# A chunked RWKV-7 recurrence with top-1 expert routing: blocks fetched unit by unit, triangular inversion spread over four slots, logits summed on GpSimd, late weights behind the second gather

## The chip, the cores and the metric

The kernel runs on one core of a Trainium2 chip. The metric is the device time of one execution in microseconds (us). The core has five instruction streams: PE (TensorE: matmuls, with PEld for its weight loads), DVE (VectorE), ACT (ScalarE), POOL (GpSimd) and SP (SyncE, which here only issues DMA transfers). Each stream works through its own instructions in order and waits where a result of another stream, or a transfer, is missing. All DMA transfers run on 16 shared DMA engines.

## The reference

First comes a linear recurrence over 768 tokens for 4 batches x 8 heads, with a state matrix of 40 x 40 for each, then a routed feed-forward layer over all 3072 tokens of width 320:

```python
for t in range(S):                       # 768 tokens; r, k, v, w, a, b: (4, 8, 768, 40)
    y[:, :, t] = einsum('bhd,bhde->bhe', rt, state)
    Sa = einsum('bhde,bhe->bhd', state, at)
    state = state * wt[:, :, None, :] - einsum('bhd,bhe->bhde', Sa, bt) \
            + einsum('bhd,bhe->bhde', vt, kt)
x = y as (3072, 320)
logits = x @ w_gate                      # 8 experts
expert_idx = argmax(logits); gate_w = softmax(logits)[expert_idx]
for e in range(8):                       # only the 80 tokens of largest gate_w are kept
    out[tok_idx] = gate_w[tok_idx] * (relu(x[tok_idx] @ w1[e]) @ w2[e])
```

Tokens that are not kept stay zero in the output.

## The kernel before

**Tiling.** The sequence is cut into 12 chunks of T = 64 tokens, the batches into 2 pairs: 24 *units*, taken in the order chunk by chunk, pair by pair. A unit holds 2 batches x 8 heads x 64 tokens. The states of the two pairs take turns, so unit n needs the state that unit n - 2 left. Four consecutive units (NG = 4) make a *group*; there are six. Inside a unit the recurrence is turned into matmuls. This needs the inverse of a triangular matrix for each head, in two diagonal blocks of C = 32 tokens; the part below the diagonal is done by a matmul (`below`).

**Ahead work.** What doesn't depend on the state is made seven units ahead (AHEAD = NG + 3). In the loop over n, m = n + 7 is the unit made ahead and o = n - 1 the unit that is finished. `decays`, `forward` and `backward` turn `w` into running products (a PE transpose, an ACT copy, DVE scans). `turned_a`/`decayed_a`, `doubled`/`inverted` and `operand` make the scaled factors. `system` multiplies them into `np`, and `system_kept` (L352) copies it to the tile `nt` on ACT, stores `nt` to the DRAM tensor `blocks` (two transfers, L355), and masks `nt` on POOL.

**Inversion of a group.** The inverses of a group's 4 x 16 head-chunks in 2 blocks are computed at once on DVE, one on each partition, with the 32 x 32 matrix along the free axis. Three steps lead there. `fetch(k)` (L365) reads the blocks of group k back from DRAM into `lt`, four transfers of 32 partitions each. `begin(k)` (L370) makes the start matrix `tt` with a mask on POOL. Thirty `step`s follow, two DVE instructions each (L381, L384). `end(k)` writes `tt` to the DRAM tensor `solved` (L387) and reads it back, transposed, as `dt` (L392). `diagonal` uses `dt` as matmul weights from the first unit of the next four slots on.

**Order of the work.** The order on each engine is written out by hand. Everything goes through `do`, which ties each new instruction to the one before it on the same engine, SP among them, so each engine's order is the order of the text. In the loop the places are, for unit n: `decays(m+1)`, `turned(o)`, `system(m)`, the scans, `together` (matmuls with v and with the state), `right`, `system_kept(m)`, the fetch (in n % 4 == 0 only, for the group just completed), `doubled`, `right_kept`, `turned_a(m+1)`, `lower(o)`, `diagonal(n, 0)`, `inverted(m+1)`, `reads_g`, `below`, then the list of inversion steps, `logits(o-1)`, `turned_r`, `diagonal(n, 1)`, `operand(m+1)`, `summed(o)` (which writes the new state at L522 and `xT` at L526), `logits_summed(o-1)`. Every input load is issued by SP right behind the operation that frees its single buffer (`raw_w`, `raw_a`, `raw_s`, `raw_r`; `v` has three).

The inversion steps wait in a list `steps` with a cost in us for each. `pause(steps, x)` takes steps from it until their costs exceed x. Before the change, `begin` stands in slot 0 of a group (n % 4 == 0), and `invert`, which fills the list, at the end of that slot; the steps then run in slots 1 and 2 (6.7 us each, besides 0.7 us earlier in each slot) and 3 (the rest). In the last group, where nothing is made ahead any more, the amounts are 9 and 5.5.

**Start.** `prepare` makes units 0 to 6 ahead before the loop. The first group's inversion runs there in full, with nothing else on DVE.

**Gate.** `logits` multiplies `xT` with a picking matrix that holds the gate weights, copies the result to `xb` and stores the token rows to `x_rows`; `logits_summed` adds its four parts (L552, DVE). `gate` turns four units of logits into probabilities; the largest 80 gate weights of each expert are found with lists of maxima on DVE.

**Routing and experts.** After the loop, POOL splits ids and gates into bf16 pieces (`pieces`), DVE and PE find each kept token's slot and row number, `keep_at_work` runs 40 filler matmuls (L146), and POOL gathers the rows of the first four experts (L932). SP loads the expert weights: experts 0 to 2 before that, then a small transfer `held`, which reads the row numbers `idx_g` (L983), then experts 3 to 7. Each expert is `tokens` (transposes, L942/L944), `first_half` (L955, L962), `second_half` (L972) and an indirect store (L975).

Of the kernel before, what the change touches and what calls it, by code (L numbers as in the profile page):

```python
# [18 lines left out]
def kernel(  # L19
# [26 lines left out]
    nc = tc.nc  # L46
# [19 lines left out]
    assert G * ZT == 512 and NG * 32 == 128 and E == 8 and 1 <= cap <= 128  # L66
# [66 lines left out]
    ones_b = const.tile([128, 128], BF16, name="ones_b")  # L133
    behind_b = const.tile([128, 128], BF16, name="behind_b")
    seg_t = const.tile([128, E, 2 * NM], F32, name="seg")
    seg = seg_t.rearrange("p e m -> p (e m)")
    iot = const.tile([128, 1, cap], F32, name="iot")


# [7 lines left out]

    nc.gpsimd.tensor_copy(ones_b, ones)
    nc.gpsimd.tensor_tensor(out=behind_b, in0=strict, in1=ones, op=Alu.subtract)
    nc.gpsimd.memset(seg_t, 1.0)  # L150
    nc.gpsimd.memset(seg_t[:, :, 0:1], 0.0)
    iot_i = const.tile([128, cap], I32, name="iot_i")
    nc.gpsimd.iota(iot_i, pattern=[[1, cap]], base=1, channel_multiplier=0)
    nc.gpsimd.tensor_copy(iot[:, 0, :], iot_i)


    with ExitStack() as p1:
# [202 lines left out]
        def fetch(k):  # L360
            inverse[k]["lt"] = lt = sb.tile([128, C * C], F32, name="lt", tag="lt")
            for i in range(Z):
                for j in range(NS):
                    m = block(i, j)
                    nc.sync.dma_start(lt[m].rearrange("p (s t) -> p s t", s=C),  # L365
                                      blocks[k, m, :, :, j * C : (j + 1) * C].rearrange("s u h t -> (u h) s t"))
# [183 lines left out]
        def logits_summed(n):  # L550
            i = share_of[n]
            nc.vector.tensor_reduce(logit[i][:, n - shares[i][0], :], of[n]["xb"][:, :, 2 * D :].rearrange("p g e -> p e g"),  # L552
                                    axis=AX, op=Alu.add)
            of[n].clear()
# [137 lines left out]
        def joined(n):  # L692
            do(operand, n)
            do(system, n)
            do(system_kept, n)

        def prepare(n, before=None, next_=True):
# [10 lines left out]
            if before is not None:  # L708
                do(system, before)
                do(system_kept, before)  # L710
            if next_:
# [11 lines left out]
        do(fetch, 0)  # L723
# [18 lines left out]
        for n in range(NU + 2):  # L742
# [24 lines left out]
            if coming:  # L767
                do(system_kept, m)
                if m % NG == NG - 1:
                    do(fetch, m // NG)  # L770
# [25 lines left out]
            if not coming:  # L796
                pause(steps, 9 if n % NG == 1 else 5.5 if n % NG == 2 else 100)
                pause(rounds_, LISTS.get(n, 0))
            elif n % NG == 0:
                do(begin, m // NG)  # L800
            else:
                pause(steps, 6.7 if n % NG < NG - 1 else 100)
# [218 lines left out]
```

## Time and profile before

| what | value |
|---|---|
| median of 3 runs | 620.11 us (618.28 to 622.42) |
| profiled execution | 620.17 us |
| its span, first to last instruction | 618.5 us |
| mean granted TensorE clock | 0.871 |
| busy: PE / PEld / DVE / ACT / POOL | 480.6 / 411.2 / 362.5 / 234.7 / 130.2 us |

Time by stage in the profiled execution (us from the start; clock is the granted share of TensorE's full clock):

| stage | from : to | length | PE busy | DVE busy | clock | DMA share |
|---|---|---|---|---|---|---|
| start, units 0 to 4 made ahead | 0 : 49.8 | 49.8 | 29.96 | 35.52 | 0.97 | 0.63 |
| first inversion, rest of the start | 49.8 : 98.8 | 49.0 | 16.93 | 30.45 | 0.55 | 0.52 |
| units n = 0 to 3 | 98.8 : 164.2 | 65.4 | 58.09 | 44.12 | 0.90 | 0.55 |
| n = 4 to 7 | 164.2 : 236.4 | 72.2 | 65.50 | 48.27 | 0.88 | 0.68 |
| n = 8 to 11 | 236.4 : 302.3 | 65.9 | 57.62 | 48.81 | 1.00 | 0.68 |
| n = 12 to 15 | 302.3 : 368.0 | 65.7 | 58.98 | 45.49 | 0.95 | 0.53 |
| n = 16 to 19 | 368.0 : 425.5 | 57.5 | 46.72 | 38.74 | 0.94 | 0.43 |
| n = 20 to 23 and the last reads | 425.5 : 476.5 | 51.0 | 43.90 | 29.02 | 0.97 | 0.18 |
| end of the gate | 476.5 : 497.5 | 21.0 | 5.80 | 18.39 | 0.58 | 0.08 |
| routing, first gather | 497.5 : 526.2 | 28.7 | 10.07 | 16.65 | 0.59 | 1.01 |
| first experts | 526.2 : 551.4 | 25.2 | 24.67 | 0.81 | 0.59 | 1.06 |
| remaining experts | 551.4 : 618.5 | 67.1 | 62.31 | 6.26 | 0.98 | 0.24 |

How to read it: a line of the trace gives the start, the length, the engine, the line of the kernel, the operation, and what it writes and reads; in brackets stand the idle time of the engine just before it and what ended that idle time. "SPq" is SP's queue of DMA issues; the length there is the time that the issue took, not the transfer. A matmul's end is modelled, so a busy PE isn't PE at its peak.

### The profile page before, as it was taken

The numbers are of one execution on the slowest core, as the hardware profiler recorded it, in microseconds if no ns is written. First come the engines' busy times: TensorE is split into PE (matmuls) and PEld (weight loads), VectorE is DVE, ScalarE is ACT, GpSimd is POOL, SyncE is SP. The second block draws the span as 40 slices with busy tenths as digits, with TensorE's granted clock in tenths as the row PEclk, the third lists the DMA queues.
The fourth block names the chain that finished last, engine by engine and source line by source line (L and its number), as shares of the span: only waits on it lengthen the run. The fifth ranks groups of instructions, "written<-read, shape, count | busy, mean of one in ns | idle before, by whom it ended". The sixth has DMA issues, their size and how long they took to land. (4 is left out here: it accounts for less than half of the span.)

```text
span 618.5 us, 25228 instructions
## 1 busy us (share of the span) xinstructions
PE 480.6 (78%) x11281; PEld 411.2 (66%) x11281; DVE 362.5 (59%) x870; ACT 234.7 (38%) x418; POOL 130.2 (21%) x171
## 2 busy tenths in 40 slices
PE   2874039978979898978998898599888205999996
PEld 1653037867869787877887787488777204877874
DVE  8766932678547874888567853988266984001010
ACT  2462015645654655655564554154445000000000
POOL 5022003222221412422231133021112012111011
PEclk9986557989996989999998899799999556579999
DMA  4587077535777658765766345125210179995000
GB/s 75 109 165 134 11 122 124 95 64 116 137 122 145 133 128 153 144 140 96 141 113 121 73 87 103 33 70 79 49 33 14 21 258 347 330 334 158 14 14 14
DMA packets 236033, 71.46 MB, mean 116 GB/s; under 512 B 217236, under 2 KB 228756, under 8 KB 235924
## 3 DMA queue, kind: packets, MB, share of 16 engines
q1 hardware_dynamic: 223728, 66.47, 49.6%
q10 hardware_dynamic: 11428, 1.73, 1.7%
q8 instruction: 89, 1.46, 0.9%
q0 software_dynamic: 768, 1.64, 0.9%
q14 instruction: 20, 0.16, 0.1%
HBM read 51.69 MB, written 18.12 MB: 113 GB/s over the span
## 5 line engine op out<-in xcount | busy, mean ns | idle before, releaser
L272 POOL TENSOR_SCALAR_AFFINE_SELECT side<-side 64x1024 f32<-64x1024 f32 x47 | 55.3, 1176 | 113.0 <-ACT side L500 111.7
L384 DVE TENSOR_TENSOR tt<-tt,tmp 128x30 f32<-128x30 f32 (+9 forms) x180 | 71.2, 396 | 6.6
L381 DVE TENSOR_TENSOR tmp<-tt,lt 128x30 f32<-128x30 f32 (+9 forms) x180 | 65.2, 362 | 14.5 <-POOL tt L370 9.3
L272 POOL TENSOR_SCALAR_AFFINE_SELECT nt<-nt 64x512 f32<-64x512 f32 x48 | 34.4, 717 | 139.6 <-ACT nt L352 138.3
L416 PE MATMUL yp<-rT,gT 64*64 64x64 f32 x768 | 30.6, 231 | 35.9 <-DVE lg L552 28.2
L416 PEld LDWEIGHTS yp<-rT,gT 64*64 64x64 f32 x768 | 27.7, 145 | 37.8 <-issue 35.6
L319 ACT COPY qd<-qt 128x1024 f32<-128x1024 f32 x24 | 25.3, 1053 | 71.6 <-DVE qt L305 68.1
L974 DVE TENSOR_SCALAR y<-yp,weight 80x320 f32<-80x320 f32 x8 | 4.4, 548 | 79.4 <-PE yp L972 79.4
L522 DVE TENSOR_TENSOR state<-yp,pt 64x320 f32<-64x320 f32 x44 | 21.4, 487 | 50.1 <-PE yp L518 49.8
L518 PE MATMUL yp<-side,scaled 128*64 128x128 f32 (+1 forms) x768 | 47.5, 279 | 2.2 <-POOL side L272 2.2
L245 PE MATMUL tp<-ident,raw_a 128*128 128x128 f32 x96 | 19.2, 333 | 35.4 <-DMA raw_a<-in_a_dram 35.0
L518 PEld LDWEIGHTS yp<-side,scaled 128*64 128x64 f32 x768 | 41.9, 143 | 3.9 <-POOL side L272 2.4
L298 DVE TENSOR_TENSOR_SCAN pt<-decay,begins 128x520 f32<-128x520 f32 x24 | 30.3, 1263 | 20.2 <-ACT decay L292 20.0
L453 PE MATMUL pr<-yy,dt 32*32 32x40 f32 x1536 | 39.0, 203 | 3.7 <-ACT yy L446 1.8
L453 PEld LDWEIGHTS pr<-yy,dt 32*32 32x32 f32 x1536 | 32.6, 111 | 10.9 <-issue 5.7
L972 PE MATMUL yp<-w,hT 128*80 128x320 f32 x128 | 38.5, 448 | 0.0
L245 PEld LDWEIGHTS tp<-ident,raw_a 128*128 128x128 f32 x96 | 12.4, 166 | 38.5 <-issue 34.7
L966 ACT ACTIVATE hT<-hp 128x320 f32<-128x320 f32 x16 | 6.1, 434 | 83.3 <-PE hp L962 83.3
L955 PEld LDWEIGHTS hp<-xe,w 128*128 128x128 f32 x256 | 36.2, 227 | 1.5 <-issue 0.2
L955 PE MATMUL hp<-xe,w 128*128 128x80 f32 x256 | 36.4, 311 | 0.0
L266 PE MATMUL sp<-ahT,sT 64*64 64x64 f32 x1536 | 32.7, 241 | 2.3 <-ACT sT L342 2.3
L404 PE MATMUL pr<-side,nt 64*64 64x40 f32 x768 | 33.8, 235 | 0.4 <-issue 0.4
(300 smaller groups left out, 998.9 us busy)
## 6 DMA issues: line engine op xcount, KB each, us to landing
w<-in_moe_w_dram SPq DMA_DIRECT2D x8, 1280.0 KB, 14.1
w<-in_moe_w_dram SPq DMA_DIRECT2D x8, 1024.0 KB, 15.9
blocks<-nt SPq DMA_DIRECT2D x48, 128.0 KB, 2.5
raw_w<-in_w_dram SPq DMA_DIRECT2D x48, 80.0 KB, 3.2
raw_s<-in_b_dram SPq DMA_DIRECT2D x48, 80.0 KB, 2.9
raw_r<-in_r_dram SPq DMA_DIRECT2D x48, 80.0 KB, 3.1
side<-in_v_dram SPq DMA_DIRECT2D x48, 80.0 KB, 2.8
x_rows<-xb SPq DMA_DIRECT2D x48, 80.0 KB, 2.3
```

Source lines behind the costliest of these rows:

```text
L245: nc.tensor.transpose(p[:, g, :], t[:, g, :], ident)
L266: nc.tensor.matmul(p[i, q, z, g, :], lhsT=lhs[m, z, g, i], rhs=rhs[m, g, halves[z]], start=True, stop=True)
L272: nc.gpsimd.affine_select(out=o, in_=o, compare_op=Alu.is_gt, fill=0.0, base=0, pattern=[[0, o.shape[1]], [1, T]], channel_multiplier=-1)
L298: nc.vector.tensor_tensor_scan(flat(pt), flat(chunks(n)), flat(begins), 0.0, op0=Alu.mult, op1=Alu.add)
L381: nc.vector.tensor_tensor(out=tm, in0=t3[:, 0:i, i : i + 1].to_broadcast([128, i, n]), in1=l3[:, i : i + 1, i + 1 :].to_broadcast([128, i, ...
L384: nc.vector.tensor_tensor(out=t3[:, 0:i, i + 1 :], in0=t3[:, 0:i, i + 1 :], in1=tm, op=Alu.add)
L404: yield lambda h=h, z=z: nc.tensor.matmul(pr[halves[1 - z], h, :], lhsT=o["nt"][halves[z], z, of_head(n, h), :], rhs=vu[halves[z], z, h, 0:D],
L416: yield lambda z=z, g=g, m=m: nc.tensor.matmul(y[m, z, g, 0:T], lhsT=o["gT"][m, z, g, :], rhs=o["rT"][m, g, halves[z]], start=g == 0, stop ...
L453: nc.tensor.matmul(o["pr"][m, h, :], lhsT=dt_[m, (n % NG) * 2 * G + of_head(n, h), :], rhs=o["yy"][m, h, :], start=h == 0, stop=True, skip ...
L518: nc.tensor.matmul(o["y"][m, z, g, 0 : T if last else T + HB], lhsT=o["s"][:, z, 2 * g + q, :], rhs=x, start=False, stop=True, skip_group_ ...
L955: nc.tensor.matmul(hp[f // (FK // 2)][:, f % (FK // 2), :], lhsT=t1[:, i, f * 128 : (f + 1) * 128], rhs=xe[:, i, :], start=f % (FK // 2) = ...
L972: nc.tensor.matmul(yp, lhsT=hT[:, f, :], rhs=w2[:, f, :], start=f == 0, stop=f == FK - 1)
```

## The change

The change has five parts.

1. **Fetch by unit.** `fetch` now takes a unit n in place of a group. It reads that unit's quarter of the blocks into `lt` (eight partitions for each of four transfers), directly after `system_kept` of the same unit, in the start and in the loop. `lt` gets two buffers.
2. **Steps in four slots.** In slot 0, `invert` and `pause(steps, 3)` follow `begin` at once; slots 1 and 2 take 4.9 instead of 6.7. The last group's amounts become 8 and 5.
3. **Logits on POOL.** For the first 20 units `logits_summed` is two additions on POOL instead of one reduction on DVE.
4. **Constants.** `ones_b`, `behind_b`, `seg` and `iot`, which only the routing reads, are made on POOL after the loop, behind `pieces`, in a pool of their own (`gp`) that also holds `pieces` and `rest`.
5. **Late weights.** `held` reads the rows that the second gather delivered (`rows[1]`) instead of `idx_g`, so SP issues the weights of experts 3 to 7 only after that gather has landed. The fillers grow from 40 to 52.

```diff
-        def fetch(k):
-            inverse[k]["lt"] = lt = sb.tile([128, C * C], F32, name="lt", tag="lt")
+        def fetch(n):
+            k, u = n // NG, n % NG
+            if u == 0:
+                inverse[k]["lt"] = sb.tile([128, C * C], F32, name="lt", tag="lt", bufs=2)
             for i in range(Z):
                 for j in range(NS):
                     m = block(i, j)
-                    nc.sync.dma_start(lt[m].rearrange("p (s t) -> p s t", s=C),
-                                      blocks[k, m, :, :, j * C : (j + 1) * C].rearrange("s u h t -> (u h) s t"))
+                    x = m.start + 2 * G * u
+                    nc.sync.dma_start(inverse[k]["lt"][x : x + 2 * G].rearrange("h (s t) -> h s t", s=C),
+                                      blocks[k, m, u, :, j * C : (j + 1) * C].rearrange("s h t -> h s t"))
...
         def logits_summed(n):
             i = share_of[n]
-            nc.vector.tensor_reduce(logit[i][:, n - shares[i][0], :], of[n]["xb"][:, :, 2 * D :].rearrange("p g e -> p e g"),
-                                    axis=AX, op=Alu.add)
+            lg, x = logit[i][:, n - shares[i][0], :], of[n]["xb"][:, :, 2 * D :]
+            if n < NL:
+                part = sb.tile([128, G // 2, E], F32, name="part", tag="part")
+                nc.gpsimd.tensor_tensor(out=part, in0=x[:, 0 : G // 2], in1=x[:, G // 2 :], op=Alu.add)
+                nc.gpsimd.tensor_tensor(out=lg, in0=part[:, 0], in1=part[:, 1], op=Alu.add)
+            else:
+                nc.vector.tensor_reduce(lg, x.rearrange("p g e -> p e g"), axis=AX, op=Alu.add)
...
         # in joined(n) and, for `before`, in prepare(n, before):
             do(system_kept, n)
+            do(fetch, n)
...
         # in the start:
-        do(fetch, 0)
         do(begin, 0)
...
         # in the loop:
             if coming:
                 do(system_kept, m)
-                if m % NG == NG - 1:
-                    do(fetch, m // NG)
+                do(fetch, m)
...
             if not coming:
-                pause(steps, 9 if n % NG == 1 else 5.5 if n % NG == 2 else 100)
+                pause(steps, 8 if n % NG == 1 else 5 if n % NG == 2 else 100)
                 pause(rounds_, LISTS.get(n, 0))
             elif n % NG == 0:
                 do(begin, m // NG)
+                invert(m // NG)
+                pause(steps, 3)
             else:
-                pause(steps, 6.7 if n % NG < NG - 1 else 100)
+                pause(steps, 4.9 if n % NG < NG - 1 else 100)
...
-            if coming and m % NG == NG - 1:
-                invert(m // NG)
...
 +    ones_b = gp.tile([128, 128], BF16, name="ones_b")
+    behind_b = gp.tile([128, 128], BF16, name="behind_b")
+    seg_t = gp.tile([128, E, 2 * NM], F32, name="seg")
+    iot = gp.tile([128, 1, cap], F32, name="iot")
+    nc.gpsimd.tensor_copy(ones_b, ones)
+    nc.gpsimd.tensor_tensor(out=behind_b, in0=strict, in1=ones, op=Alu.subtract)
+    nc.gpsimd.memset(seg_t, 1.0)
+    nc.gpsimd.memset(seg_t[:, :, 0:1], 0.0)
+    nc.gpsimd.iota(iot_i, pattern=[[1, cap]], base=1, channel_multiplier=0)
+    nc.gpsimd.tensor_copy(iot[:, 0, :], iot_i)
...
-        keep_at_work(ps_l, "still", 40, late)
+        keep_at_work(ps_l, "still", 52, late)
...
-    held = nc.dram_tensor("held", (cap, E), I32, kind="Internal")
-    nc.sync.dma_start(held[:, :], idx_g)
+    held = nc.dram_tensor("held", (cap, E), F32, kind="Internal")
+    nc.sync.dma_start(held[:, :], rows[1][:, 0:E])
     for e in range(3, E):
         weights_of(e)
```

## The prediction

> **What bounds the kernel now.** I read the table of stages first, then the queue of SyncE in one group of units, then the chain around one fetch, then the tail. Unit n runs from one copy `yy<-pr` on ACT to the next; a unit with n divisible by 4 is slot 0 of its group. Columns of the stage table: start:end, length, then busy time (and count) of PE, PEld, DVE, ACT, POOL, granted clock, DMA share, GB/s.
>
> ```profile
> 250.60:269.20 18.60, 14.72 (x448) 13.18 (x448) 15.50 (x36) 9.30 (x16) 6.88 (x10) 1.00 0.66 135
> 269.20:286.00 16.80, 14.61 (x451) 12.80 (x448) 14.60 (x30) 9.34 (x16) 3.83 (x4) 1.00 0.64 132
> 286.00:300.40 14.40, 13.88 (x442) 12.37 (x442) 10.91 (x27) 8.41 (x16) 2.28 (x2) 1.00 0.64 132
> 300.40:315.80 15.40, 14.43 (x445) 12.61 (x445) 7.76 (x18) 10.46 (x19) 4.28 (x6) 1.00 0.71 116
> ```
>
> These are slots 1, 2, 3 and the next slot 0. Slots 1 and 2 carry most inversion steps, have DVE busy for 15 us and are 2 to 3 us longer; slots 3 and 0 stand at 14.4 and 15.4 us, near PE's own 14. A second limit shows only in the queue of SyncE (start, length, line, transfer):
>
> ```profile
> 264.88 1.24 SPq L548 DMA_DIRECT2D x_rows<-xb  x2
> 266.21 1.31 SPq L212 DMA_DIRECT2D raw_r<-in_r_dram  x2
> 267.63 2.07 SPq L212 DMA_DIRECT2D side<-in_v_dram  x2
> 269.79 0.59 SPq L660 DMA_DIRECT2D out_dram<-zero  x1
> 270.47 1.58 SPq L212 DMA_DIRECT2D raw_w<-in_w_dram  x2
> 272.15 1.26 SPq L355 DMA_DIRECT2D blocks<-nt  x2
> 273.50 1.71 SPq L212 DMA_DIRECT2D raw_a<-in_a_dram  x2
> 275.30 0.60 SPq L212 DMA_DIRECT2D raw_s<-in_k_dram  x1
> ```
>
> Each start is the end before it plus 0.1 us: SyncE issues 17 transfers a unit without a pause, about 0.8 us each with gaps, 13.0 to 13.7 us a unit. Slots 0 and 3 add the fetch and the `solved`/`dt` transfers. Over n = 8 to 11 (65.9 us) SyncE is short of work for under 5 us, all but 1.2 of it waits for transfers to land. It is already the fullest queue, and it runs late, as one fetch shows:
>
> ```profile
> 234.53 0.99 ACT L352 COPY nt<-sp 128x1024 f32<-128x1024 f32 x1
> 241.21 1.22 SPq L355 DMA_DIRECT2D blocks<-nt  x2
> 243.72 2.94 SPq L365 DMA_DIRECT2D lt<-blocks  x4
> 245.94 0.99 DVE L522 TENSOR_TENSOR state<-yp,pt 64x320 f32<-64x320 f32 x2 [5.73 <-PE yp L518]
> 249.83 1.76 POOL L370 TENSOR_SCALAR_AFFINE_SELECT tt<-lt 128x1024 f32<-128x1024 f32 x1 [9.56 <-DMA lt<-blocks]
> ```
>
> `nt` is ready at 235.5, its store is issued 5.7 us later, the fetch waits 1.3 us for the store to land, and `begin` on POOL starts at 249.83, **after** DVE's state update of that unit. Before the change nobody needs `begin` until slot 1.
>
> **The Trainium skill.** "DMA: Bandwidth & Descriptors", section "Two DMAs through the same engine are not ordered", says that a read of what another DMA wrote must wait at the issuing engine for the completion semaphore; the 1.3 us gap before 243.72 is that wait, with all of SyncE's queue behind it. Section "Issuing engines are not separate DMA queues" calls issue time usually small beside the transfer; here 17 issues fill a unit, so the trace decides. "TensorE: Matmul & The Clock Gate", Part 1, says that an idle window of some 3.4 us halves the clock; the trace agrees: 0.55 granted over 49.8 to 98.8 us, where PE is busy for 17 of 49 us.
>
> **The change, part by part.** The sum is made against the profiled execution: 620.17 us, span 618.5 and 1.7 around it; the median of the three runs is 620.11, the same.
>
> *Fetch by unit.* Per group, 4 fetch issues become 16, each of a quarter. Four issues took 2.13 to 2.96 us; from below, the first of each four takes 0.31, so 1.4 us. I take 2.3, since issue time hardly follows size (80 KB loads and 128 KB stores all take 0.6). The wait ahead was 1.3 to 2.8 us; I take 1.3. So 3.6 us of SyncE in each of slots 1, 2, 3, and nothing new in slot 0. Behind it stand `raw_a`, `raw_s`, `x_rows`, `raw_r`, `v`, `raw_w` and the next store; from the end of its issue to PE's use a load of `raw_a` has 3.4 us for n = 9 (248.1 to 251.5), 10.2 for n = 11 (275.2 to 285.4). SyncE's time for n = 8 to 11 becomes 65.9 - 1.2 + 3 x 3.6 = **75.5 us**.
>
> *Steps in four slots.* DVE spends 22.7 us a group on 60 step instructions (136 us over six groups). Spread evenly, a slot has 5.7 beside 6.1 of other DVE work, and slot 3 shows that 4.6 us of steps cost nothing: all four units would run at about 15.2 us, 60.8 a group, **5 us less** than 65.9. But slot 0's six steps stand in DVE's order ahead of the state update and now wait for `begin`. From the store's issue: 8.6 us to `begin` (241.21 to 249.83), less 0.8 for the smaller fetch, plus 1.4 for the mask with its memset of 0.15, plus 3.5 for six steps (the six equal-sized ones that end the first inversion): **12.9 us**. The state update came 4.7 us after that issue, so DVE is 8.2 us late; at n = 4, 12, 16 the same sum gives 9.4, 8.1, 8.3. Behind the waiting DVE are state, xT and the next scans; PE's next state matmuls wait for xT. Each us by which SyncE falls further behind is added; with units of 15.2 against SyncE's 16.7, 16.7 and about 23.7 (slot 3), it is 4 to 5 more, so a stall of 13.
>
> So the groups: n = 0 to 3 has no state update in slot 0 and a SyncE with 17 us idle, -2. n = 4 to 7: 60.8 + 13 = 74 to 75 against 72.2 (which held 13.7 us of half clock), +2.5. n = 8 to 11: 75.5 against 65.9, +9.6. n = 12 to 15: 60.8 + 13, and 3 for a PE that goes to half clock in the stall, against 65.7, +11. n = 16 to 19: stall 8.3, less 3 for steps moved out of n = 17 (20.6 us now), plus 3 of clock, +8. **Loop: +29.**
>
> *Start.* Units 0 to 3 are made every 5.9 us with SyncE busy for about 4.9; with 3.6 more they take 8.3. Three such intervals are +7, less 2.5 because only a quarter is fetched after the last: **+4.7** until `begin(0)`, and all that follows waits for it. The later fetches (units 4, 5) fall where SyncE waits from 61.7 to 77.4: nothing; without that cover 7.
>
> *POOL's constants.* Six instructions, 0.28 + 0.44 + 0.41 + 0.10 + 0.19 + 0.24 = 1.7 us, leave the start, where DVE's 8-element cast lasts 3.75 us, until POOL's memsets are over: **-1.5** (from 0 to -1.7). At the end they run from 499.9, and the first reader starts at 509.94: nothing.
>
> *Logits on POOL.* Two adds of at most 0.24 us (the row of `ids`) on a POOL that is 21% busy, read by the gate three units later: nothing. DVE loses 0.2 us in 20 units, inside the stalls: nothing.
>
> *Tail.*
>
> ```profile
> 516.91 6.45 PE L146 MATMUL still_p<-late 128*128 128x256 bf16 x40
> 526.23 0.33 PE L942 MATMUL xp<-ident,rows 80*128 80x80 f32 x2 [2.87 <-DMA rows<-x_rows,idx_g]
> 528.08 7.12 PE L955 MATMUL hp<-xe,w 128*128 128x80 f32 x32
> 553.11 3.69 PE L955 MATMUL hp<-xe,w 128*128 128x80 f32 x32
> ```
>
> The same 32 matmuls take 7.12 us, later 3.69: after the 2.87 us gap PE ran at half clock from 527.7 to 548.2. Twelve more fillers of 0.16 us last until 525.3. The gather took 6.75 us among weight loads against 3.7 when alone (the last one); with the late weights held back it lands 0.6 to 1.6 us earlier, so the gap is about nil: **-1.5**, and if the clock holds, half of 20.5 us more: **-10**. The late weights start some 8 us later but end near 570, and expert 7 is first needed at 601: nothing. From both sides the tail is 0 to -12; I take the kept clock, -11.5, at 6 in 10.
>
> Sum: 29 + 4.7 - 1.5 - 11.5 = +20.7, so **641 us**.
>
> **The rivals.** *Forecast* (0.62): SyncE and the wait for `begin` eat the balance; 630 with a smaller lag to 652 with a cold tail. *Worse* (0.13): each stall costs a half-clock stretch beyond what I count, 3.5 us in four groups, and the tail stays cold: 641 + 10 + 14 = 665. For it: the unit from 178.7 ran at clock 0.71 and took 23.3 us. *Wash* (0.13): SyncE has hidden slack and the lag at slot 0 stays at 5.7, a stall of 8: group 69, loop about +12, 620 + 12 + 3 - 11.5 = 624. *Faster* (0.12): the spread steps pay. The place is slot 0, the price is the stall, which is the lag of the store plus 2.5 us; the gain is 5 a group, so it decides at a lag of 2.5 us. With no lag: four groups at -2.5, tail -11.5, start +3: 602. Against it: lags of 8.6, 5.7, 5.0 and 5.1 us at the four stores today, with less in SyncE's queue than after.
>
> **How the numbers follow.** A measurement of this kernel can tell about 1% from no change. Faster by over 1% (under 614) is the last case, 0.11; within 1% is most of the wash, 0.11; slower 0.78. The range 616 to 664 leaves out the faster case and half of the worse one.
>
> **What would show it.** Right: in slot 0, DVE's first step waits for POOL's mask and the state update starts some 13 us after the store's issue; SyncE without a pause in the groups from n = 4 on; groups near 75 us; units 1 to 3 of a group near 15 to 17; a gap before the first gathered transposes under 1 us. Wrong: fetch issues well under 0.5 us, stores issued within 2 us of `nt`, and slot 0 as short as the others; then the kernel is faster.

## The result and the profile after

The changed kernel takes **647.5 us** (median of 4 runs, 644.1 to 655.2) against 619.8 before, 28 us more. The ratio, taken without the slow run of 655.2 us, which is also the profiled one, is 1.042 with a 95% interval of 1.035 to 1.050. The forecast was 641, range 616 to 664.

The profiled execution took 655.15 us (span 653.4). A second profiled execution of the same kernel, in the last series of experiments, took 647.87 us (span 646.2) and stands closer to the median. Time by stage, each from its first `yy<-pr` copy on ACT to the next stage's, in us:

| stage | before | after | after, again | forecast of the difference |
|---|---|---|---|---|
| start, up to n = 0 | 98.8 | 110.9 | 112.2 | +3.2 |
| n = 0 to 3 | 65.4 | 62.3 | 67.8 | -2 |
| n = 4 to 7 | 72.2 | 75.8 | 75.2 | +2.5 |
| n = 8 to 11 | 65.9 | 77.4 | 76.7 | +9.6 |
| n = 12 to 15 | 65.7 | 73.1 | 72.7 | +11 |
| n = 16 to 19 | 57.5 | 60.7 | 61.0 | +8 |
| n = 20 to 22 | 39.0 | 39.4 | 38.7 | 0 |
| from n = 23 to the end | 153.9 | 153.9 | 141.9 | -11.5 |

So, against the span before, the loop costs 23.0 or 26.4 us (forecast 29), the start 12.1 or 13.4 (forecast 3.2), and the tail 0 or -12 (forecast -11.5). For the second execution, 620.2 + 26.4 + 13.4 - 12.0 = 648.0.

The table of stages of the first execution, units n = 8, 9, 10, 11 (slots 0 to 3); start:end, length, busy time (count) of PE, PEld, DVE, ACT, POOL, granted clock, DMA share, GB/s:

```profile
249.03:279.28 30.25, 17.42 (x402) 15.39 (x395) 9.84 (x23) 9.65 (x19) 6.29 (x10) 0.73 0.71 141
279.28:296.05 16.77, 16.03 (x504) 14.13 (x507) 14.42 (x29) 9.34 (x17) 6.20 (x7) 0.97 0.58 114
296.05:311.09 15.04, 14.61 (x459) 12.85 (x452) 12.49 (x26) 9.45 (x18) 5.03 (x6) 1.00 0.65 96
311.09:326.40 15.31, 14.42 (x458) 12.70 (x452) 11.30 (x29) 9.38 (x19) 3.87 (x7) 1.00 0.58 111
```

Slots 1 to 3 did become more even, at about 15 to 17 us with DVE busy for 11 to 14. Slot 0 pays for it: 30 us in which no engine is busy for more than 17.4. What happens there is seen in the order of time (start, length, engine, line, what it writes and reads; in brackets the idle time ahead of it and what ended that):

```profile
247.16 0.99 ACT L337 COPY nt<-sp 128x1024 f32<-128x1024 f32 x1
...
259.87 1.25 SPq L340 DMA_DIRECT2D blocks<-nt  x2
262.40 2.13 SPq L354 DMA_DIRECT2D lt<-blocks  x4
...
267.40 1.27 POOL L359 TENSOR_SCALAR_AFFINE_SELECT tt<-lt 128x1024 f32<-128x1024 f32 x1 [14.50 <-DMA lt<-blocks]
268.70 0.19 DVE L370 TENSOR_TENSOR tmp<-tt,lt 128x30 f32<-128x30 f32 x1 [10.43 <-POOL tt L359]
...
273.01 0.98 DVE L511 TENSOR_TENSOR state<-yp,pt 64x320 f32<-64x320 f32 x2
```

`nt` is ready at 248.15, its store is issued 11.7 us later, the mask starts 7.5 us after the store's issue, DVE stands for 10.43 us at the first step, and the state update comes 13.1 us after the store's issue (forecast 12.9; at n = 4, 12 and 16 it is 14.6, 13.5 and 13.6). The list of waits of the same execution (engine, line, what it waited for: us in total, times, longest) shows the two ends of this stall:

```profile
DVE tmp L370 <- POOL tt L359: 48.9, 5, 14.3
...
PE yp L405 <- DVE xT L515: 38.5, 13, 10.0
...
PE pr L442 <- DMA dt<-solved: 11.2, 6, 3.8
```

Five of the six masks hold DVE for 48.9 us in all. One of the five is the start's (4.4 us); at n = 12 DVE stands 11.4 us at the same step, which the list puts down to a load. PE's state matmuls stand for 38.5 us behind the `xT` that DVE then owes. The third line is a wait that the kernel before doesn't have: PE stands for the solved blocks at the first `diagonal` of a group.

### The profile page after: what moved, and what is told of

Same layout as the page of the kernel before. It is cut to its first block, busy times and chain, and to the rows that moved or that the text cites. A ratio compares the mean times of both kernels' runs of the same rounds, so it can differ in the third digit from the quotient of the medians.

```text
span 653.4 us, 25378 instructions
## 1 busy us (share of the span) xinstructions
PE 493.2 (75%) x11293; PEld 422.0 (65%) x11293; DVE 360.5 (55%) x850; ACT 235.3 (36%) x418; POOL 149.4 (23%) x211
## 5 line engine op out<-in xcount | busy, mean ns | idle before, releaser
L370 DVE TENSOR_TENSOR tmp<-tt,lt 128x30 f32<-128x30 f32 (+9 forms) x180 | 66.9, 372 | 65.4 <-POOL tt L359 48.9
L257 POOL TENSOR_SCALAR_AFFINE_SELECT nt<-nt 64x512 f32<-64x512 f32 x48 | 43.9, 915 | 138.2 <-ACT nt L337 137.0
L405 PE MATMUL yp<-rT,gT 64*64 64x64 f32 x768 | 31.9, 239 | 44.9 <-DVE xT L515 38.5
L405 PEld LDWEIGHTS yp<-rT,gT 64*64 64x64 f32 x768 | 29.1, 153 | 45.9 <-issue 40.0
L442 PE MATMUL pr<-yy,dt 32*32 32x40 f32 x1536 | 39.3, 203 | 16.3 <-DMA dt<-solved 11.2
L442 PEld LDWEIGHTS pr<-yy,dt 32*32 32x32 f32 x1536 | 32.8, 111 | 24.4 <-issue 10.2
L318 DVE TENSOR_TENSOR scaled<-raw_s,pp 128x320 f32<-128x320 f32 x48 | 21.2, 482 | 35.4 <-PE pp L316 29.0
L979 PE MATMUL yp<-w,hT 128*80 128x320 f32 x128 | 39.4, 457 | 0.0
L230 PE MATMUL tp<-ident,raw_w 128*128 128x128 f32 x96 | 19.8, 343 | 21.8 <-DMA raw_w<-in_w_dram 21.8
L393 PE MATMUL pr<-side,nt 64*64 64x40 f32 x768 | 36.3, 242 | 0.0
```

Source lines behind the costliest of these rows:

```text
L230: nc.tensor.transpose(p[:, g, :], t[:, g, :], ident)
L257: nc.gpsimd.affine_select(out=o, in_=o, compare_op=Alu.is_gt, fill=0.0, base=0, pattern=[[0, o.shape[1]], [1, T]], channel_multiplier=-1)
L370: nc.vector.tensor_tensor(out=tm, in0=t3[:, 0:i, i : i + 1].to_broadcast([128, i, n]), in1=l3[:, i : i + 1, i + 1 :].to_broadcast([128, i, ...
L393: yield lambda h=h, z=z: nc.tensor.matmul(pr[halves[1 - z], h, :], lhsT=o["nt"][halves[z], z, of_head(n, h), :], rhs=vu[halves[z], z, h, 0:D],
L405: yield lambda z=z, g=g, m=m: nc.tensor.matmul(y[m, z, g, 0:T], lhsT=o["gT"][m, z, g, :], rhs=o["rT"][m, g, halves[z]], start=g == 0, stop ...
L442: nc.tensor.matmul(o["pr"][m, h, :], lhsT=dt_[m, (n % NG) * 2 * G + of_head(n, h), :], rhs=o["yy"][m, h, :], start=h == 0, stop=True, skip ...
```

## Experiments

Each is timed against the kernel before on the same chip. There the kernel before took 622.4 us in the first series (four kernels), 617.9 in the second and 617.3 in the third. Groups are given as n = 4 to 7, 8 to 11 and 12 to 15, from the profiled execution; the kernel before has 72.2, 65.9 and 65.7, the changed one 75.8, 77.4 and 73.1.

### The fetch by unit alone

The kernel before with part 1, and with the constants moved so that two `lt` buffers have room:

```diff
-                if m % NG == NG - 1:
-                    do(fetch, m // NG)
+                do(fetch, m)
```

> The kernel before with the fetch by unit alone (the constants move too, since the second buffer of the fetched blocks needs their space; worth -1.5 us). Steps stay in slots 1 to 3. Theory Q (SyncE's queue sets the groups' time): each group from n = 4 on carries three more fetches, some 3 us each with their waits, so groups of 66 us become 73 to 74; with +12 in the start the time is 640 to 648 us. Theory B (in the changed kernel it was DVE's wait for the start mask in slot 0 that set the groups' time, and SyncE only kept pace): groups stay at 65 to 67 us and only the start is longer: 630 to 634 us.

Measured: 646.6 us, ratio 1.044 (1.034 to 1.054). Start 112.0, groups 74.0, 74.5, 65.8. In the 74.0 us of n = 4 to 7 the queue of SyncE holds 57.1 us of issues, 5.4 of gaps between them and 10.9 of waits for stores and `solved` to land, 73.4 together. **The queue is full for the whole group**, and so it is for n = 8 to 11: there SyncE stands for only 0.4 of the 74.5 us for anything but a landing, counting gaps of over 0.15 us between its issues (the forecast's sum for that group was 75.5). The group n = 12 to 15 carries the same fetches and takes 65.8 us, as before, against what theory Q expected of it. There the kernel before has 42.9 us of issues, not 55.6 as for n = 8 to 11, and SyncE stands 11.5 us for the last inversion step: its queue had room. But even where it is full, the loss is not spread over the slots. The table of stages for n = 8 to 11:

```profile
249.20:271.40 22.20, 20.23 (x444) 18.15 (x438) 6.57 (x13) 9.57 (x18) 6.70 (x8) 0.69 0.77 129
271.40:289.20 17.80, 14.95 (x417) 13.13 (x410) 14.70 (x36) 9.48 (x18) 4.23 (x6) 0.91 0.64 118
289.20:307.20 18.00, 15.90 (x446) 14.12 (x446) 14.61 (x30) 9.38 (x17) 3.66 (x4) 0.90 0.64 124
307.20:323.70 16.50, 15.52 (x504) 13.71 (x506) 12.67 (x33) 9.36 (x19) 3.29 (x5) 1.00 0.53 112
```

Slot 0 has PE busy for 20.2 us at a clock of 0.69 and takes 22.2, where it took 15.1 (236.4 to 251.5) before. Slots 1 to 3 are 1.5 us longer together. What happens at the start of that slot, in order of time:

```profile
239.21 0.21 DVE L373 TENSOR_TENSOR tt<-tt,tmp 128x30 f32<-128x30 f32 x1
...
244.01 0.57 SPq L376 DMA_DIRECT2D solved<-tt  x1
247.26 2.15 SPq L381 DMA_DIRECT2D dt<-solved  x4
...
251.72 0.99 PE L442 MATMUL pr<-yy,dt 32*32 32x40 f32 x24 [1.47 <-DMA dt<-solved]
```

The last inversion step ends at 239.4, but SyncE comes to `solved` only 4.6 us later; in the kernel before it is there at once:

```profile
227.42 0.21 DVE L384 TENSOR_TENSOR tt<-tt,tmp 128x30 f32<-128x30 f32 x1
227.66 0.51 SPq L387 DMA_DIRECT2D solved<-tt  x1
```

So `dt` lands late, PE stands for it 2 us in two pieces, and 13.7 us of half clock follow. How much of the group's loss is this half clock, and how much the full queue would cost without it, is not separated. For n = 12, where `solved` is issued 2.3 us behind its last step, slot 0 takes 18.6 us with 3.4 of half clock, and the group stays at 65.8.

### The steps in four slots alone

The kernel before with part 2; the fetch stays one for each group:

```diff
                 do(begin, m // NG)
+                invert(m // NG)
+                pause(steps, 3)
             else:
-                pause(steps, 6.7 if n % NG < NG - 1 else 100)
+                pause(steps, 4.9 if n % NG < NG - 1 else 100)
```

> The kernel before with the steps in four slots alone; the fetch stays one for each group, in slot 0. Theory Q: DVE's balance pays while SyncE has no more to do: groups of 61 to 63 us, 600 to 608 us in all. Theory B: DVE stands in slot 0 until the mask is made, some 14 us after the issue of the store, 8 to 9 us late in each group: groups of about 70 us, first one 2 us shorter, start as before: 628 to 636 us.

Measured: 636.4 us, ratio 1.021 (1.008 to 1.034). Groups 74.6, 74.9, 69.3; slots 0 at 27.7, 27.7, 24.5 us, slots 1 to 3 at 13.9 to 16.5. In its list of waits:

```profile
DVE tmp L381 <- POOL tt L370: 65.6, 6, 15.0
PE yp L416 <- DVE lg L552: 52.8, 16, 11.8
```

(`lg` is the short sum that stands right behind `xT` in DVE's order.) **The wait for the mask does set slot 0**, without any extra fetch in SyncE's queue. Each of the two parts alone brings n = 8 to 11 from 65.9 to 74 or 75; together they bring 77.4. The two don't add up, since the one hides behind the other: during the stall SyncE works off its queue. At n = 10 and 11 the stores of the blocks stand 7.5 and 4.7 us behind their copies with part 1 alone, and 1.9 and 2.1 us in the changed kernel. In the changed kernel SyncE stands for something other than a landing for only 2.1 us in each of the groups n = 4 to 7 and 8 to 11, so its queue sets nearly the same time as the stall; in n = 12 to 15 it is 9.3 us, and the stall sets the time.

### More fillers alone

```diff
-        keep_at_work(ps_l, "still", 40, late)
+        keep_at_work(ps_l, "still", 64, late)
```

> The kernel before with 64 fillers in place of 40, so that they end at about the landing of the first gather (9.2 us after their start). If the gap before the first gathered transposes is what sends TensorE to half clock for 20.5 us: -8 to -10 us, 610 to 612 us. If the experts' own matmuls behind the fillers bring the half clock anyway, or the fillers delay the first expert: 619 to 622 us.

Measured: 613.5 us, ratio 0.984 (0.972 to 0.996). In the profiled execution the clock was still lost: the gap ahead of the first gathered transposes is down to 0.33 us, but the rows of the second gather come 1.24 us late, and 17.1 us of half clock follow; from n = 23 to the end it takes 153.1 us. So the fillers alone don't secure the tail, and the median's gain isn't explained by this profile. Two of the four runs took 608.9 and 610.9 us at a granted clock of 0.895 and 0.896, the profiled one 616.1 at 0.885; that those two kept the clock in the tail is possible, and not shown.

### The changed kernel with one fetch for the first group

In the start, the first group's blocks are fetched at once behind its fourth unit, with the four transfers of the kernel before:

```diff
             k, u = n // NG, n % NG
+            if k == 0:
+                if u < NG - 1:
+                    return
+                inverse[k]["lt"] = lt = sb.tile([128, C * C], F32, name="lt", tag="lt", bufs=2)
...
+                return
```

> The changed kernel with one fetch of all four units for the first group, in the start; everything else as changed. If the unit fetches in the start cost what the trace suggests (first mask 11.7 us later, partly because loads wait for a completion semaphore that a fetch holds): loop begins at 97 to 99 us instead of 110.9, and the time is 11 to 13 us below the changed kernel, 633 to 636 us. If the start is bound otherwise: less than 4 us.

Measured: 642.8 us, ratio 1.035 (1.024 to 1.046). The start is 99.5 us, 11.4 to 12.7 less than in the two executions of the changed kernel: **the fetches in the start cost all that the start had lost.** Groups 78.6, 70.3, 72.6. The profiled execution's span, 641.7, is only 4.5 below the 646.2 of the second execution, because its tail lost the clock (a gap of 1.06 us ahead of the gathered transposes, 153.2 us from n = 23 to the end against 141.9); the rest is -12.7 in the start and -3 in the loop.

### The steps of slot 0 behind the state update

```diff
                 do(begin, m // NG)
-                invert(m // NG)
-                pause(steps, 3)
...
             if past:
                 do(summed, o)
+            if coming and n % NG == 0:
+                invert(m // NG)
+                pause(steps, 3)
```

> The changed kernel, with the steps of slot 0 issued behind the unit's state update and xT and no longer ahead of them. Theory Stall (DVE stands at the first step until the mask has come, and PE's next state matmuls wait for DVE): the state update of n = 4, 8, 12, 16 then comes some 5 us after the store's issue instead of 13 to 14.6, and the slot-0 units fall from 24 to 30 us to 17 to 20; groups n = 4 to 15 then stand at what SyncE's queue alone sets, 73 to 74 us as with the fetch by unit alone, and the kernel at 635 to 640 us. Theory Queue alone (the groups are 74 to 77 us because SyncE has that much to issue; the wait for the mask only decides in which unit the time falls): the slot-0 units shrink, but slots 1 to 3 grow by as much, groups stay within 1.5 us of 75.8, 77.4 and 73.1, time 643 to 650 us.

Measured: 647.4 us, ratio 1.052 (1.043 to 1.060); groups 77.1, 72.4, 74.7. Neither theory has it all. The state update no longer waits for the mask (at n = 8 it starts 4.3 us after the store's issue), but the time is the same, and slot 0 is still 25 to 27 us. In order of time, around n = 9:

```profile
268.73 0.99 DVE L511 TENSOR_TENSOR state<-yp,pt 64x320 f32<-64x320 f32 x2 [6.72 <-PE yp L507]
273.70 0.19 DVE L370 TENSOR_TENSOR tmp<-tt,lt 128x30 f32<-128x30 f32 x1 [3.27 <-POOL tt L359]
...
279.53 1.24 DVE L290 TENSOR_TENSOR_SCAN qt<-decay,ends 128x520 f32<-128x520 f32 x1
280.80 1.05 ACT L304 COPY qd<-qt 128x1024 f32<-128x1024 f32 x1 [8.71 <-DVE qt L290]
281.76 0.42 ACT L435 COPY yy<-pr 128x320 f32<-128x320 f32 x1
```

DVE still stands 3.27 us for the mask. Behind the steps come the next unit's scans, ACT's copy of `qt` waits for them 8.71 us, and right behind that copy in ACT's order stands `yy<-pr`, for which PE waits (6.5 us). **The stall moved from PE's state matmuls to PE's diagonal.** In both places in slot 0 that were tried, something needed soon stands behind these steps. And the other limit remains: in the 72.4 us of n = 8 to 11 SyncE stands for only 0.4 us for anything but a landing, so there its full queue sets the time.

### The store of the blocks on ACT's queue

```diff
-                nc.sync.dma_start(blocks[n // NG, m, n % NG], nt[m, 1 - i])
+                nc.scalar.dma_start(blocks[n // NG, m, n % NG], nt[m, 1 - i])
```

> The changed kernel, with the store of each unit's blocks issued by ACT, behind the copy that fills it, and no longer by SyncE. Theory Lag (the store stands 6 to 12 us behind its copy in SyncE's queue, and everything from the fetch to the mask and the slot-0 steps is late by that): the store leaves within 0.5 us of the copy's end, SyncE has 1.3 us a unit less to issue, the mask of slot 0 begins 5 to 10 us sooner, slot-0 units fall to 17 to 21 us, groups n = 4 to 15 to 66 to 70 us, and the time to 622 to 630 us. Rival (the landing of store and fetch, some 8 us from store to mask, is what counts, and the fetch still waits for its turn in SyncE's queue): the fetches keep their times, groups stay at 74 to 77 us, time 643 to 650 us. Third: ACT's own queue now waits for transfers, and PE for ACT: slower than 650 us.

Measured: 670.5 us, ratio 1.085 (1.071 to 1.100); groups 85.3, 82.5, 77.7. All three expectations missed the place. The store leaves at once (0.03 us after the copy in every unit), yet the mask of n = 8 starts 22.0 us after the store's issue instead of 7.5. SyncE waits at loads that have nothing to do with the blocks:

```profile
SPq L197 <- DMA blocks<-nt: 72.3, 17, 9.3
SPq L537 <- DMA blocks<-nt: 19.1, 7, 6.2
```

```profile
255.34 1.97 SPq L197 DMA_DIRECT2D raw_s<-in_b_dram  x2
262.07 0.60 SPq L197 DMA_DIRECT2D raw_s<-in_k_dram  x1
```

Between these two issues SyncE stands for 4.76 us. The trace names for every transfer the semaphore that it raises when it has landed:

```
start    issued by   transfer            semaphore
254.70   SyncE       raw_s<-in_k_dram    107
255.34   SyncE       raw_s<-in_b_dram    108
256.67   SyncE       raw_s<-in_b_dram    109
259.42   ACT         blocks<-nt          100
259.91   ACT         blocks<-nt          102
262.07   SyncE       raw_s<-in_k_dram    100
```

Eight semaphores (100, 102 and 104 to 109) are taken in turn by the transfers of SyncE **and** ACT, in the order of the program. So the last load of `raw_s` waits until ACT's store, eight places ahead of it, has been issued and has landed. ACT in turn issues it only behind its own copies, which wait for PE. Behind SyncE then stand `solved` and `dt`, for which PE waits 26.6 us in all here (11.2 in the changed kernel).

### The late parts alone, with 64 fillers

The kernel before with parts 4 and 5:

```diff
-        keep_at_work(ps_l, "still", 40, late)
+        keep_at_work(ps_l, "still", 64, late)
...
-    nc.sync.dma_start(held[:, :], idx_g)
+    nc.sync.dma_start(held[:, :], rows[1][:, 0:E])
```

> The kernel before with only the late parts of the change: constants of the gather made at the end, late weights held behind the second gather, and 64 fillers in place of 52. Theory Gap (PE goes to half clock for some 20 us because it stands idle for more than a microsecond at the first gathered transposes; 52 fillers left 1.3 us of that): the fillers now end with the rows landed, no gap over 0.5 us, no half clock afterwards, the first two experts take 9 to 10 us less, and with 1.4 us less in the start the kernel takes 607 to 610 us. Rival (the half clock comes whatever the fillers do, since it was still there with 64 fillers and the weights not held): 616 to 621 us.

Measured: **606.9 us**, ratio 0.983 (0.975 to 0.991). PE goes from the fillers into the gathered transposes without a gap:

```profile
513.80 9.81 PE L139 MATMUL still_p<-late 128*128 128x256 bf16 x64
523.72 0.33 PE L945 MATMUL xp<-ident,rows 80*128 80x80 f32 x2
...
524.91 3.80 PE L958 MATMUL hp<-xe,w 128*128 128x80 f32 x32
```

The 32 matmuls take 3.80 us where they took 7.12, and from n = 23 to the end it is 144.9 us instead of 153.9. All three profiles with the weights held back and 64 fillers, this one and two below, kept the clock. The start, however, is 100.1 us and no shorter than the 98.8 before: DVE's first scan does start at 8.26 instead of 9.67 and the first store of blocks leaves at 23.7 instead of 25.4, but the fourth leaves at 43.2 (43.1 before). The constants' 1.4 us are lost again within four units.

### Late parts, late steps and ACT's store together

The kernel of the run before this, with part 2, its slot-0 steps behind the state update, and the store on ACT:

```diff
             if past:
                 do(summed, o)
+            if coming and n % NG == 0:
+                invert(m // NG)
+                pause(steps, 3)
...
+                nc.scalar.dma_start(blocks[n // NG, m, n % NG], nt[m, 1 - i])
```

> The same late parts as in the run of the tail, with the fetch by group as in the kernel before, the inversion steps in all four slots, those of slot 0 behind the state update, and the stores of the blocks issued by ACT. Theory Balance (without the wait for the mask ahead of the state update and without the store's place in SyncE's queue, four even slots of 15 to 16 us pay): groups n = 4 to 15 at 61 to 64 us against 65.7 to 72.2 before, 10 to 15 us less in all, and with the tail 595 to 602 us. Rival (the other DVE work, the loads and PE set the groups, 65 to 67 us, even with the steps spread): within 3 us of the run of the tail, 605 to 611 us.

Measured: 630.5 us, ratio 1.021 (1.012 to 1.029); groups 73.9, 74.8, 72.1, slots 0 and 1 at 20 to 23 us with 4 to 14 us of half clock each. Both expectations failed. Here SyncE stands 46.6 us for ACT's stores at its input loads, and PE 23.7 us for `yy<-pr`: the two causes of the two runs above. With these in the way, that an even spread could pay is not shown.

### No fetch waits for a store

The changed kernel, in which each fetch reads a table of zeros; the inversion then works on zeros and the diagonal part of the result is left out:

```diff
-                                      blocks[k, m, u, :, j * C : (j + 1) * C].rearrange("s h t -> h s t"))
+                                      nothing[:, :, :].rearrange("s h t -> h s t"))
```

> The changed kernel, with every fetch of a unit's blocks reading, in the same shape, a small table of zeros in DRAM that is written once at the start. The blocks are still stored, but no fetch waits for a store; the inversion then works on zeros, so the diagonal part of the result is left out. Theory Store wait (SyncE stands 1.2 to 2.8 us at each fetch for the store to land, and the mask of slot 0 comes late by that): SyncE has 1.2 to 2.8 us a unit less, groups n = 4 to 15 fall from 75.8, 77.4, 73.1 to 68 to 71, the stores of the first units in the start come every 7.5 to 8.5 us instead of every 10.5, start at 102 to 104 us, time 622 to 630 us. Theory Issue (the number of issues and the eight completion semaphores that SyncE's and ACT's transfers share are the cost): in the start the intervals stay at 9.5 us or more, groups fall by 2 us at most, time 638 to 645 us.

Measured: 631.8 us, ratio 1.026 (1.016 to 1.037); start 107.8, groups 71.8, 74.6, 72.0. Each theory is half right. Against the second execution of the changed kernel the spans differ by 16.1 us: 4.4 in the start, 6.2 in the three groups, and 5.5 in n = 0 to 3, by which the two executions of the changed kernel differ too. The stores of the start still come every 10.0 us on the mean, so most of what the start lost isn't the wait for a store. And slot 0 stays at 24.5 to 28 us for n = 4, 8 and 12. In order of time, at n = 8:

```profile
249.63 1.26 SPq L344 DMA_DIRECT2D blocks<-nt  x2
250.94 1.75 SPq L358 DMA_DIRECT2D lt<-nothing  x4
...
257.68 1.26 POOL L363 TENSOR_SCALAR_AFFINE_SELECT tt<-lt 128x1024 f32<-128x1024 f32 x1 [11.95 <-DMA raw_s<-in_k_dram]
```

The fetch is issued 1.3 us behind the store instead of 2.5, but the mask starts 8.0 us after the store's issue, not sooner than the 7.5 with the wait: from the end of the issues it takes 5.0 us, 2.9 before. It isn't so everywhere. At n = 4, 12 and 16 the mask starts 7.4, 8.2 and 7.6 us after the store's issue, against 8.9, 8.1 and 8.9 in the first execution of the changed kernel. So at most 1.6 us of this lag goes. Whether the small fetches queue behind the store on the DMA engines or land slowly by themselves was not tried.

### The changed kernel, once more

Nothing is changed in it, so there is no edit.

> The changed kernel itself, once more. With the gap ahead of the first gathered transposes at 1 us or more the tail runs at half clock and lasts 153 to 154 us from n = 23 on; with a gap under 0.5 us it keeps its clock and lasts 142 to 145 us. If 52 fillers leave the gap to chance, the times lie in two groups some 9 us apart, between 640 and 656 us; if they never suffice, all lie at 644 to 656 and the profiled tail is 153 us again. The groups repeat within 2 us.

Measured: 649.3 us (647.9 to 657.8), ratio 1.052 (1.042 to 1.061). The groups repeat within 1 us, except n = 0 to 3 (67.8 against 62.3). This time the tail kept its clock:

```profile
555.86 7.29 PE L139 MATMUL still_p<-late 128*128 128x256 bf16 x52
563.81 0.33 PE L949 MATMUL xp<-ident,rows 80*128 80x80 f32 x2 [0.67 <-DMA rows<-x_rows,idx_g]
...
564.99 3.80 PE L962 MATMUL hp<-xe,w 128*128 128x80 f32 x32
```

In the first profiled execution it had not:

```profile
561.38 0.33 PE L949 MATMUL xp<-ident,rows 80*128 80x80 f32 x2 [1.32 <-DMA rows<-x_rows,idx_g]
...
562.60 6.39 PE L962 MATMUL hp<-xe,w 128*128 128x80 f32 x32
```

Of the seven profiles with the late weights held back and 52 fillers, five kept the clock (141.9 to 143.1 us from n = 23 to the end) and two lost it (153.2 and 153.9). **With 52 fillers it is left to chance.** Over all fourteen profiles of this case, the tail kept its clock in the eight where PE stood at most 0.84 us around the first gathered transposes, and lost it in the six with 1.06 us or more. The times of the runs don't fall into two clear groups, so this can't be read from them alone.

### Fillers in the stall of slot 0

```diff
+            if n % NG == 1 and coming:
+                do(keep_at_work, ps_t, "t", 64)
             do(together, n, o)
```

> The changed kernel, with 64 matmuls on zeros of the kind used in the tail put on PE ahead of the first state matmuls of the units n = 1, 5, 9 and 13, where PE stands for 7 to 8 us for DVE's xT of slot 0. Theory Clock (the stall costs twice: once itself, and again in 10 to 16 us at half clock after it): the half clock of the slot-0 units is gone, they and the first unit after fall by 5 to 7 us together, groups n = 4 to 15 to 68 to 72 us, time 630 to 636 us. Rival (PE's speed is hidden behind DVE and SyncE in those units): groups within 1.5 us of 75.8, 77.4 and 73.1, time 643 to 650 us, or more where the fillers outlast the stall.

Measured: 645.8 us (639.1 to 651.3), ratio 1.043 (1.033 to 1.052), within the spread of the changed kernel's 649.3 on the same chip. Groups 78.7, 81.8, 65.3. In both profiles of the changed kernel the half clock in n = 8 comes in two spells: 6.8 us around PE's wait for `dt<-solved`, and 10.2 us in the stall. Here the first is 13.7 us long and the second is gone. The fillers take 7.16 us and end 3 us after `xT` is begun, so they also hold PE up. Slot 0 of n = 8 takes 29.1 us, as without them. This speaks for the rival (PE's clock is hidden behind DVE's wait), but with groups that scatter by 16 us it settles nothing.

### The last group's steps spread evenly

The kernel of the late parts alone, with

```diff
-                pause(steps, 9 if n % NG == 1 else 5.5 if n % NG == 2 else 100)
+                pause(steps, 6.5 if n % NG == 1 else 6.5 if n % NG == 2 else 100)
```

> The kernel of the tail's run (late parts alone, 64 fillers), with the last group's inversion steps spread 6.5 and 6.5 us over n = 17 and 18 in place of 9 and 5.5. Theory Balance in a unit without loads and stores (n = 17 has DVE busy for 17 us of 20.4, n = 18 to 22 have 9 to 11 of 12): n = 17 falls to 17 to 18 us, n = 18 and 19 rise by less than 1 us, group n = 16 to 19 at 54 to 56 us against 57.4, time 603 to 606 us. Rival (n = 19 must then hold what is left, and n = 20 waits for the solved blocks): what n = 17 wins n = 19 and 20 lose, 606 to 608 us.

Measured: **603.3 us**, ratio 0.974 (0.962 to 0.986), faster than both kernels. Unit n = 17 of the kernel it starts from, then n = 17, 18, 19 of this one, in the table of stages:

```profile
376.80:397.10 20.30, 12.50 (x347) 11.06 (x344) 16.87 (x49) 5.91 (x12) 3.96 (x5) 0.83 0.24 44
```

```profile
374.10:391.50 17.40, 13.13 (x348) 11.61 (x352) 15.04 (x44) 5.99 (x13) 3.65 (x5) 0.85 0.28 50
391.50:404.40 12.90, 11.89 (x351) 10.67 (x351) 11.30 (x27) 5.85 (x13) 2.44 (x2) 0.94 0.23 43
404.40:416.60 12.20, 11.19 (x352) 10.04 (x352) 10.59 (x28) 5.76 (x12) 2.30 (x2) 1.00 0.46 101
```

DVE's busy time in n = 17 falls from 16.87 to 15.04 us and the unit from 20.3 to 17.4; n = 18 and 19 grow by 0.9 us together. So spreading steps does pay where nothing must wait for a mask or a load. The 3.6 us between the two medians lie within their spread; the 2 us of the group are in the profile.

## Why the prediction was right, and where it was not

**Steps in four slots: right.** The mechanism was the forecast's: DVE stands at the mask ahead of the state update. The state update comes 13.1 to 14.6 us after the store's issue (12.9 forecast, though its terms as printed add up to 12.7), slots 1 to 3 take 13.9 to 16.8 us (15.2 forecast). Part 2 alone shows it. The 4 to 5 us by which SyncE was to fall further behind were less even: the store in slot 0 stands 1.7, 6.0, 4.0 and 0.4 us further behind its copy than before at n = 4, 8, 12 and 16.

**Fetch by unit: right in sum, not in its place.** Four small issues take 1.7 us on the mean of 24 units (mostly 1.5), not the 2.3 that was taken; the wait for the store is 40.1 / 24 = 1.7 us, not 1.3. With 3.4 in place of 3.6 in three slots the step's own sum is 74.9 for n = 8 to 11, and the run of part 1 alone has 74.5. The forecast looked at the loads that stand behind the fetch; what PE missed first was `dt`, whose `solved` stands behind it too. In the changed kernel `solved` is issued 6.3 us after the last step in the group of n = 4 to 7 (0.03 before), and PE's wait for it comes on top of the wait for the mask. Where the queue had room, n = 12 to 15, part 1 alone cost nothing.

**The groups:** +23.0 or +26.4 against +29. The largest miss is n = 16 to 19, +3.2 or +3.5 instead of +8: slot 0 is 10.9 us longer there, but n = 17 falls from 20.6 to 12.2, so the steps moved out of it were worth 8.4 and not the "3 for steps moved out of n = 17". For n = 12 to 15 the sum was 4 us too high.

**Start: wrong.** "With 3.6 more they take 8.3" is the step that failed (4.9 and 3.6 are 8.5, but that is not the miss); the stores of units 0 to 3 come every 10.5 us. The queue of SyncE before, and after:

```profile
31.46 1.22 SPq L355 DMA_DIRECT2D blocks<-nt  x2
32.78 1.38 SPq L212 DMA_DIRECT2D raw_w<-in_w_dram  x2
34.94 0.59 SPq L212 DMA_DIRECT2D raw_s<-in_k_dram  x1
```

```profile
34.32 1.22 SPq L340 DMA_DIRECT2D blocks<-nt  x2
36.83 1.49 SPq L354 DMA_DIRECT2D lt<-blocks  x4
38.42 1.83 SPq L197 DMA_DIRECT2D raw_w<-in_w_dram  x2
42.60 0.59 SPq L197 DMA_DIRECT2D raw_s<-in_k_dram  x1
...
44.66 2.04 SPq L340 DMA_DIRECT2D blocks<-nt  x2
```

The forecast counted the 1.3 us ahead of the fetch and its issue. It did not count that the next loads wait as well: 0.53 us inside `raw_w`, for a fetch to land, and 2.3 us before 42.60, for a load of `raw_s` on ACT's queue, each eight transfers ahead in the turn of the semaphores (the run with the store on ACT's queue has them). Four more transfers a unit use up that turn sooner. In the profile these waits for completion come to some 10 us in the start against 3.5 before. That one fetch for the group removes the loss is shown (99.5 us), and that taking the store's wait away removes 3 to 4 us of it; how the rest is shared between issue time and the semaphores was only read from the trace. **Constants:** the -1.5 is there at the first store and gone at the fourth, so at the end of the start it is 0.

**Logits on POOL: 0**, as forecast as far as can be seen: the two additions of 0.2 us each stand behind the mask on POOL and nothing is seen to wait for them. It wasn't tried alone.

**Tail: right in size, and a matter of chance as stated.** A kept clock and the shorter gap are worth 12 us (11.5 forecast, 6 in 10; five of seven profiles had it). The first profiled execution fell on the other side. The term of the earlier landing (0.6 to 1.6 us) held in one of the two: the first transposes start 9.3 us after the fillers before, 9.4 and 8.0 after.

In the second execution, start and constants make 13.4 - 3.2 = 10.2 us of miss upwards, and loop and tail -2.6 and -0.5. That is the distance of 641 from 648. The start's cost was put at a quarter of what it is; the total came near because the rest was nearly right in sum.

## What to carry to other kernels

Work moved into an earlier, emptier slot is only free if its inputs are there: ask when its last producer lands, and what stands behind it on its engine, and behind that on the engines that wait. A queue that is full for a whole stage takes no more transfers, however small; count the waits for completion with the issues. And where a stage starts cold, cover the gap with work that lasts past the latest landing seen, and hold back the transfers that compete with it: those two, with the constants and with 64 fillers in place of the change's 52, are worth 11 us here.

## What was not expected of the hardware

- In this kernel's program the transfers issued by SyncE and by ACT share eight completion semaphores in the order of the program. A store moved to ACT's queue held SyncE's input loads for 72.3 us in one execution. A second issuing engine was no second queue.
- In the tail, a gap of 1.06 or 1.32 us on PE, with matmuls at once behind it, was followed by about 20 us of half clock; with a single gap of 0.84 us or less, none followed. This is no rule of the gap's length: in the kernel before, at n = 9, PE stands for 3.00 us up to 266.44 and no half clock follows (the clock is 1.00 for all of n = 8 to 11). The Trainium skill ("TensorE: Matmul & The Clock Gate", Part 1) lets the clock return after about one busy window of 3.4 us. Here, behind the gap of 1.32 us, the half clock lasted from 563.4 for 20.48 us, six such windows, with PE busy throughout by the trace. The measurement decides; why it took six, and why these gaps cost the clock and that one didn't, is open.
- Taking the wait for the store away saved little of the lag. The trace has 1.2 to 2.8 us of that wait for each unit; without it the mask came at most 1.6 us sooner after the store's issue, and at n = 8 not at all.
